# A stored normalised copy of the rows between the first spectral layer and the first convolution

## The chip, the core and the metric

The kernel runs on one core of a Trainium2 chip. Its time is the device time of one execution in microseconds (us). The engines of the core run their own instruction queues: TensorE (PE, matmuls; PEld is its weight loads), VectorE (DVE), ScalarE (ACT), GpSimd (POOL) and SyncE (SP), on whose queue nearly all DMAs are issued here. Each engine takes its instructions in order.

## The reference

Four layers act on x of 2048 rows by 512 columns, float32. Layers 1 and 3 are spectral, layers 2 and 4 are long convolutions along the rows, and each is added to its input.

```python
def _layernorm(x, axis=-1, eps=1e-5):
    m = jnp.mean(x, axis=axis, keepdims=True)
    v = jnp.var(x, axis=axis, keepdims=True)
    return (x - m) / jnp.sqrt(v + eps)
def _A_ref(x, w_r, w_i):
    X = rfft2(x)
    return irfft2(X * (w_r + 1j * w_i), s=(S, D))
def _B_ref(u, log_A_real, A_imag, C_real, C_imag, log_dt, D_skip):
    dt = exp(log_dt)
    A = -exp(log_A_real) + 1j * A_imag
    C = (C_real + 1j * C_imag) * dt[:, None]
    P = exp((A * dt[:, None])[:, :, None] * pos[None, None, :])
    K = 2.0 * einsum("dn,dnl->dl", C, P).real
    ...
    return y + u * D_skip[None, None, :]
x = x + _A_ref(_layernorm(x), ...)
x = x + _B_ref(_layernorm(x), ...)
x = x + _A_ref(_layernorm(x), ...)
x = x + _B_ref(_layernorm(x), ...)
```

`y` in `_B_ref` is the causal convolution of u with K, by FFTs of twice the length. K depends on the weights alone, and both convolution layers use the same.

## The kernel before

The 2048 rows lie as 128 partitions by 16 rows each, so that "a row" below is a tile of 128 x 512 (256 KB), and there are 16 of them (`n2` from 0 to 15). All transforms are matmuls with tables.

The first spectral layer (`layer_a` with `x=None`) has three parts. `spread` loads the rows, normalises them and transforms along the rows. `middle` transforms along the columns, multiplies with the weights w, and goes back. `end` folds (`fold`) and brings back each row (`rows_back`): the old row is loaded again into a tile `hr` (queue key R, L410), one matmul (L596) makes the layer's output, VectorE adds the two into `hr` (L602), and the sum is stored to an array `h1` in HBM (L604). Rows are taken in groups of 4, 4, 4, 2, 1, 1 (`LN` read from the back is their sizes), and for each group `layer_norm_stats` makes the mean and the inverse deviation: one BN_STATS (L341) and one BN_AGGR (L342) a row, then thirteen small VectorE instructions (L347 to L364, three Newton steps) that depend on each other almost throughout. They go to a small tile `norms` of 2 x 16 numbers per partition. The tile `hr` shares four buffers with the weight tile `wt` (`hr="wt"`, `WT = 4`).

The first convolution (`layer_b` with `src=hd`) works through four blocks of 128 columns. For each, `forward_norm` loads four rows' 128 columns at a time from `h1` into a tile `w` (key N, L1059), GpSimd scales and shifts each of the four with its numbers from `norms` (L1065, 64 steps in all), and `forward_b` transforms them: 32 matmuls per four rows (L318, through `side_by_side`), a copy by ScalarE (L643), and eight transposes by VectorE (L649) per block. `weigh` multiplies with the convolution kernel's spectrum (L954, L956, then sums L965 and L966 on GpSimd, mostly), `back` returns, and the sum with the rows of `h1` (L990 loads them, L994 adds) goes to `h2` or to the tile `za`, with the statistics of the next layer (L999).

Beside that, the convolution kernel itself is made: `kernel_time` builds K in time and stores it to `kt`, in groups of four units of two halves. Each half takes two matmuls, a rounding by VectorE (L833), a third matmul (L834), three ScalarE activations (L795: `kf`, then two sines into `qp`), three VectorE products (L852 twice, L854 once) and sixteen small matmuls (L865); a group begins with eight exponentials by ScalarE into `mag` (L795) of which GpSimd makes a third part (L816, L817), and ScalarE loads another table of functions before the sines and again before the exponentials. `kernel_freq` transforms K block by block, with the same `forward_b`, and its product is kept (`keep`, L919).

The order of the work on each engine is not written out. The program lists steps interleaved by shares (`interleave`, `FILL`, `FS`), and a planner that runs a timeline of its own orders each engine's instructions from that list; a step moves ahead when what stands before it would have to wait. Buffers are taken in rotation: a tile's next use waits until all readers of its earlier use are done.

Of the kernel before, what the change touches and what calls it, by code (L numbers as in the profile page):

```python
# [31 lines left out]
LAGE = 3  # L32
WT = 4
WA = 7
LN = '444211'
# [3 lines left out]
NEWT = 1  # L39
XNE = 'gggg'  # L40
GA = '22444'
# [22 lines left out]
S2 = 0  # L64
# [184 lines left out]
class Net:  # L249
# [134 lines left out]

    def layer_a(self, w, x=None, src=None, dst=None):

# [179 lines left out]
        def fold(n2):  # L566
            if n2 == 0:
                vs["tat"] = self.load("ta" if x is not None else TT, "tat", [16, 128])
                if x is not None:
                    self.xn = self.sb("x", [16, 512])  # L570
                else:
                    self.norms = self.sb("norms", [2, 16])
            p = self.ps("p3", [512])
# [19 lines left out]
        def rows_back(n2):  # L593
            old = row(n2, self.sb("hr", [512])) if x is None else x[:, n2]
            p = self.ps("p3", [512])
            nc.tensor.matmul(p, vs["tat"][:, n2], vs.pop(n2), start=True, stop=True)  # L596
            if not done:
                norm["sums"] = self.sb("lsum", [4], 2)
            if S2 if x is None else S3:
                self.add_up(old, old, p, norm["sums"][:, len(done):len(done) + 1])  # L600
            else:
                nc.vector.tensor_add(old, old, p)  # L602
            if x is None:
                self.dma("D")(dst[:, n2], old)  # L604
            done.append(old)
            if len(done) == sizes[-1]:
                sizes.pop()
                n = len(done)
                nr = self.layer_norm_stats(done, newton=x is None or NW[2] == "1", sums=norm["sums"][:, :n] if (S2 if x is None else S3) else None,
                                           nr=self.norms[:, :, n2 - n + 1:n2 + 1] if x is None else None)  # L610
# [323 lines left out]

    def layer_b(self, kf, T, out, x=None, src=None, first=None, more=(), fill=(), switch=(), kept=None, after=None):

# [30 lines left out]
        def back(blk, Y):  # L967
# [15 lines left out]
            def rows(n0):  # L983
# [13 lines left out]
                if src is not None:  # L997
                    for i in range(4):
# [3 lines left out]

        steps = [first or self.forward_norm(0, T, src)] + [self.forward_norm(blk, T, src, "z3" if more and blk == 3 else "z")
                                                           for blk in range(1, 4)]
# [44 lines left out]

    def forward_norm(self, blk, T, h=None, tag="z"):  # L1050

        ds = slice(128 * blk, 128 * blk + 128)
        rows = {}

        def src(n2):
            i = n2 % 4
            if i == 0:
                t = rows["t"] = self.sb("w", [4, 128])
                self.dma("N")(t, h[:, n2:n2 + 4, ds])  # L1059
                for k in range(4):  # L1060
                    scale, bias = (self.norms[:, c, n2 + k:n2 + k + 1] for c in (1, 0))
                    if XNE[k] == "a":
                        self.nc.scalar.activation(t[:, k], t[:, k], ACT.Identity, bias=bias, scale=scale)
                    else:
                        (self.nc.gpsimd if XNE[k] == "g" else self.nc.vector).tensor_scalar(  # L1065
                            t[:, k], t[:, k], scale, bias, op0=ALU.mult, op1=ALU.add)
            return rows["t"][:, i]

        return self.forward_b(src if h is not None else lambda n2: self.xn[:, n2, ds], T, tag)

# [5 lines left out]
def net_kernel(ctx, tc, x, w, ends, kin, log_dt, d_skip, out, **cst):  # L1076
# [14 lines left out]
    with ExitStack() as outer:  # L1091
        with ExitStack() as early:
            early.enter_context(net.phase("pk", P, pk=(2048, PK), pv=(2048, PV)))
            with net.phase("p", P, p1=(2048, 8 - PK - PV), p2="p1", p3="p1"), \
                    net.phase("a", x=(32768, 1), ta=(8192, 1), ca=(6912, 1), u=(16384, 2), w=(2056, WA), wt=(2056, WT), hr="wt",
                              wv="w", junk="w"):
                A = net.layer_a(w, src=xv, dst=hd)
                with net.phase("m", side="right", raw=(8192, 1), val=(10240, 1), tmp=(14336, 1), hp=(5120, 2)):
# [29 lines left out]
            F = [net.kernel_freq(blk, kt, d_skip, kf, kept, T) for blk in range(4)]  # L1128
            first = net.forward_norm(0, T, hd)
            at = cuts[1]  # L1130
# [25 lines left out]
            net.layer_b(kf, T, hd2, src=hd, first=first, more=[(2 * b - EF, F[b]) for b in range(EF, 4)],  # L1156
                        fill=[K[i:j] for i, j in zip(cuts, cuts[1:])], switch=[(SW, switch), (SW + 2, fetch)], kept=kept, after=after)
# [42 lines left out]
```

## Time and profile before

| | |
|---|---|
| three runs | 804.79, 809.13, 813.25 us (median 809.13) |
| the profiled execution | 813.32 us, of which 811.5 us are the span from the first to the last instruction |
| mean granted TensorE clock | 0.924 |
| DMA | 80.49 MB, of it 54.77 MB read from HBM and 25.03 MB written |

The profile names an instruction by its line (L602), engine, operation, what it writes and reads (`hr<-hr,p`), and shape. A row in order of time has its start, its duration in us, and in brackets for how long the engine had been idle and what ended that. An instruction's duration can reach into the next one's, since they are pipelined, so the distance between two starts is what a chain of them costs. A row of a table by stretch has the busy time and the number of instructions of each engine in the stretch. "Granted clock" is the share of TensorE's full clock that the throttle left. The three runs spread over 1%, and a difference is read against that.

### The profile page before, as it was taken

Reading aid. Unit: us, or ns where it says so; the run is one execution under the profiler, and the core shown is the slowest. Engines: PE = TensorE matmul, PEld = TensorE weight load, DVE = VectorE, ACT = ScalarE, POOL = GpSimd, SP = SyncE. Lnnn points to the kernel's source line nnn. Section 1 sums busy time; section 2 is a strip of 40 time slices with the busy share of each in tenths; the row PEclk is TensorE's granted clock in tenths of the full one; section 3 lists DMA queues with packets and bytes.
Section 4 is the critical chain, followed back from the end, with each engine's and each line's share of the span. In section 5 each row is a group of like instructions: output and inputs, shape, how many; then the busy total and the mean of one; then the engine's idle time right before and its main releaser. Section 6 shows DMA issues by size and latency. Waiting matters only on the chain. (4 is left out here: it accounts for less than half of the span.)

```text
span 811.5 us, 18861 instructions
## 1 busy us (share of the span) xinstructions
PE 640.9 (79%) x7231; PEld 450.0 (55%) x7232; DVE 644.8 (79%) x1307; ACT 428.4 (53%) x918; POOL 406.0 (50%) x594
## 2 busy tenths in 40 slices
PE   3448788896867977998689969665999896989895
PEld 2336666664534534654266637344877663566675
DVE  6998739789898979879796977657577796977971
ACT  2424769855548765786578714213766345323311
POOL 3675876755617054711574644180065661654752
PEclk9999989999978998999899989887999997999998
DMA  8200642253547322560335466302123013323511
GB/s 310 111 0 2 153 103 61 99 110 127 116 141 179 122 29 53 123 174 26 69 104 124 138 140 189 120 17 102 52 80 85 21 44 113 105 74 96 149 53 53
DMA packets 144609, 80.49 MB, mean 99 GB/s; under 512 B 78500, under 2 KB 124200, under 8 KB 143624
## 3 DMA queue, kind: packets, MB, share of 16 engines
q1 hardware_dynamic: 144264, 78.77, 34.6%
q8 instruction: 57, 0.93, 0.5%
q0 software_dynamic: 256, 0.52, 0.4%
q14 instruction: 32, 0.26, 0.1%
HBM read 54.77 MB, written 25.03 MB: 98 GB/s over the span
## 5 line engine op out<-in xcount | busy, mean ns | idle before, releaser
L966 POOL TENSOR_TENSOR u<-wb,wb 64x512 f32<-64x512 f32 x64 | 93.1, 1454 | 106.9 <-DVE wb L954 99.7
L318 PE MATMUL p<-z,mb 128*64 128x512 f32 (+1 forms) x480 | 105.7, 560 | 18.8 <-DVE z L649 10.4
L954 DVE TENSOR_TENSOR wb<-p,kk 128x512 f32<-128x512 f32 x128 | 80.8, 674 | 17.9 <-PE p L318 16.5
L318 PE MATMUL p<-mb,u 128*64 128x64 f32 x2048 | 78.5, 246 | 20.0 <-POOL u L965 19.5
L318 PEld LDWEIGHTS p<-mb,u 128*64 128x64 f32 x2048 | 75.2, 160 | 28.9 <-POOL u L965 23.3
L865 PE MATMUL pv<-qp 128*64 128x128 f32 x1024 | 77.8, 292 | 10.3 <-DVE qp L854 8.8
L865 PEld LDWEIGHTS pv<-qp 128*64 128x64 f32 x1024 | 61.1, 145 | 38.1 <-issue 16.8
L643 ACT COPY z<-p 128x512 f32<-128x512 f32 x96 | 51.8, 597 | 57.0 <-PE p L318 47.3
L854 DVE TENSOR_TENSOR qp<-qp,mag 128x1024 f32<-128x1024 f32 x64 | 80.4, 1260 | 0.9
L852 DVE SCALAR_TENSOR_TENSOR qp<-qp,mag 128x256 f32<-128x256 f32 x128 | 64.6, 522 | 16.6 <-ACT qp L795 16.5
L528 DVE TENSOR_TENSOR w<-wt,p 128x514 f32<-128x514 f32 x64 | 42.7, 687 | 35.8 <-PE p L318 25.6
L980 ACT COPY u<-p 128x512 f32<-128x512 f32 x64 | 37.4, 588 | 61.0 <-PE p L318 60.7
L318 PEld LDWEIGHTS p<-z,mb 128*64 128x64 f32 x480 | 37.6, 147 | 55.1 <-issue 25.1
L533 POOL TENSOR_TENSOR w<-w,w 64x257 f32<-64x257 f32 x48 | 40.4, 842 | 52.2 <-DVE w L528 47.4
L649 DVE STREAM_TRANSPOSE z<-z 128x512 f32<-128x512 f32 x96 | 58.3, 671 | 9.0 <-ACT z L643 9.0
L458 PE MATMUL p<-w,w 128*128 128x128 f32 x128 | 32.8, 438 | 40.8 <-DVE w L451 29.7
L1065 POOL TENSOR_SCALAR w<-w,norms 128x128 f32<-128x128 f32 x64 | 38.8, 619 | 37.8 <-DMA w<-h 19.2
L795 ACT ACTIVATE kf<-pk 128x512 f32<-128x512 f32 x64 | 38.9, 607 | 33.0 <-PE pk L834 30.9
L458 PEld LDWEIGHTS p<-w,w 128*128 128x128 f32 x128 | 28.5, 327 | 44.8 <-issue 23.9
L833 DVE TENSOR_SCALAR kw<-pk 128x512 bf16<-128x512 f32 x64 | 43.1, 680 | 8.2 <-PE pk L831 8.1
L795 ACT ACTIVATE qp<-kf,half 128x512 f32<-128x512 f32 x64 | 47.3, 738 | 0.1
L546 PE MATMUL p<-ca,w 128*128 128x128 f32 x256 | 41.5, 294 | 7.3 <-DVE w L535 2.5
(198 smaller groups left out, 1533.0 us busy)
## 6 DMA issues: line engine op xcount, KB each, us to landing
wt<-in_w SPq DMA_DIRECT2D x32, 257.0 KB
w<-h SPq DMA_DIRECT2D x32, 256.0 KB
kf<-kk SPq DMA_DIRECT2D x32, 256.0 KB
kk<-kf SPq DMA_DIRECT2D x32, 256.0 KB
u<-in_x SPq DMA_DIRECT2D x16, 256.0 KB
hr<-in_x SPq DMA_DIRECT2D x16, 256.0 KB
kt<-stage SPq DMA_DIRECT2D x32, 128.0 KB
h<-hr SPq DMA_DIRECT2D x16, 256.0 KB
```

Source lines behind the costliest of these rows:

```text
L318: last = self.nc.tensor.matmul(out, weights, data, start=True, stop=True, skip_group_check=True).ins
L458: nc.tensor.matmul(p[:, b], xf[:, b], t, start=True, stop=True)
L528: nc.vector.tensor_mul(m[pl], W, px[:, None, :].to_broadcast([128, 2, 257]))
L643: nc.scalar.copy(tiles["z"][:, :, :, b, m:m + 2].rearrange("p u j m r -> p (u j) (m r)"), ps[b].rearrange("p u j m r -> p (u j) (m r)"))
L649: nc.vector.transpose(tiles["zt"][:, u:u + 8].rearrange("p u j d -> p (u j d)"), tiles["z"][:, u:u + 8].rearrange("p u j b m r -> p (u j b ...
L795: last["x"] = nc.scalar.activation(*a, **k).ins
L833: nc.vector.tensor_scalar(whole, p, MAGIC, -MAGIC, op0=ALU.add, op1=ALU.add)
L852: nc.vector.scalar_tensor_tensor(QP[:, c, 0], QP[:, c, 1, :, ::-1], -1.0 if c else 1.0, m[:, 0], op0=ALU.mult, op1=ALU.mult)
L854: nc.vector.tensor_mul(t, t, mag[:, None, 1:3, 256 * j:256 * j + 256].to_broadcast([128, 2, 2, 256]))
L865: nc.tensor.matmul(p[64 * t:64 * t + 64, g], QP[:, c, 2, d:d + 2].rearrange("p s a -> p (s a)"), QP[:, c, 0:2, d:d + 2].rearrange("p k s b ...
L954: nc.vector.tensor_mul(split(m[c, pl], "du", [32, 16]), by_channel(p), split(k[c], "du", [32, 16]))
L966: e[1].tensor_add(y[64:128], v[0, 1], v[1, 0])
```

## The change

The numbers of a row's norm are applied where they are made. In the first spectral layer ScalarE writes `scale * row + bias` for each row of a group into a tile `xr` (128 x 512, two buffers), which a DMA stores to a new array `hn` in HBM; the other spectral layer did this before, into a tile that stays on the chip. The first convolution's `forward_norm` then loads from `hn` instead of `h1`, and GpSimd's 64 steps are gone, with the tile `norms`. The sums are still stored to `h1` and loaded from there for the addition. The tile `hr` gets seven buffers of its own.

```diff
+HR = 7
-XNE = 'gggg'
...
             if len(done) == sizes[-1]:
                 sizes.pop()
                 n = len(done)
-                nr = self.layer_norm_stats(done, ..., nr=self.norms[:, :, n2 - n + 1:n2 + 1] if x is None else None)
-                if x is not None:
-                    for i in range(n):
-                        nc.scalar.activation(self.xn[:, n2 - n + 1 + i], done[i], ACT.Identity,
-                                             bias=nr[:, 0, i:i + 1], scale=nr[:, 1, i:i + 1])
+                nr = self.layer_norm_stats(done, ...)
+                for i in range(n):
+                    k_ = n2 - n + 1 + i
+                    y = self.sb("xr", [512]) if x is None else self.xn[:, k_]
+                    nc.scalar.activation(y, done[i], ACT.Identity, bias=nr[:, 0, i:i + 1], scale=nr[:, 1, i:i + 1])
+                    if x is None:
+                        self.dma("D")(norm_dst[:, k_], y)
                 done.clear()
...
         def src(n2):
-            i = n2 % 4
-            if i == 0:
-                t = rows["t"] = self.sb("w", [4, 128])
-                self.dma("N")(t, h[:, n2:n2 + 4, ds])
-                for k in range(4):
-                    scale, bias = (self.norms[:, c, n2 + k:n2 + k + 1] for c in (1, 0))
-                    if XNE[k] == "a":
-                        self.nc.scalar.activation(t[:, k], t[:, k], ACT.Identity, bias=bias, scale=scale)
-                    else:
-                        (self.nc.gpsimd if XNE[k] == "g" else self.nc.vector).tensor_scalar(
-                            t[:, k], t[:, k], scale, bias, op0=ALU.mult, op1=ALU.add)
-            return rows["t"][:, i]
+            if n2 % 4 == 0:
+                rows["t"] = self.sb("w", [4, 128])
+                self.dma("N")(rows["t"], xn[:, n2:n2 + 4, ds])
+            return rows["t"][:, n2 % 4]
...
-    hd, hd2 = (net.dram.tile([128, 16, 512], F32, name=n) for n in ("h1", "h2"))
+    hd, hd2, hn = (net.dram.tile([128, 16, 512], F32, name=n) for n in ("h1", "h2", "hn"))
...
-                    net.phase("a", ..., w=(2056, WA), wt=(2056, WT), hr="wt",
+                    net.phase("a", ..., w=(2056, WA), wt=(2056, WT), hr=(2048, HR), xr=(2048, 2),
```

The planner orders anew what the change touches. The line numbers in its rows are those of the kernel that they belong to: L602, L833, L852, L854, L795, L604, L787 of before are L600, L832, L851, L853, L794, L602, L786 of the changed kernel. The first place is VectorE at the row additions of the first spectral layer. Before, the thirteenth and the fourteenth addition of the sixteen stand close together, with a little of the convolution kernel's making around them:

```order
L602 TENSOR_TENSOR hr_601_2460<-hr_601_2460,p1_602_2462 128x512
L833 TENSOR_SCALAR kw_410_1766<-pk_411_1767 128x512
L852 SCALAR_TENSOR_TENSOR qp_408_1758<-qp_408_1758,mag_365_1594 128x256 x2
L602 TENSOR_TENSOR hr_606_2477<-hr_606_2477,p1_607_2479 128x512
L342 BN_AGGR bmv_585_2404<-bst_589_2414 128x2
L583 TENSOR_TENSOR w_599_2453<-p1_597_2446,w_598_2451 128x256
L584 TENSOR_TENSOR w_599_2453<-p1_597_2446,w_598_2451 128x256
L833 TENSOR_SCALAR kw_420_1803<-pk_421_1804 128x512
```

Now the twelfth addition stands behind the end of the second group's norm (`lnn_544`) and behind a whole group of the convolution kernel's making (`qp_475` is its last):

```order
L853 TENSOR_TENSOR qp_475_2009<-qp_475_2009,mag_389_1694 128x2x512
L360 SCALAR_TENSOR_TENSOR lnr_551_2286<-lnt_552_2287,lnr_551_2286 128x4
L358 SCALAR_TENSOR_TENSOR lnt_552_2287<-lnr_551_2286 128x4
L359 TENSOR_TENSOR lnt_552_2287<-lnt_552_2287,lnv_550_2285 128x4
L360 SCALAR_TENSOR_TENSOR lnn_544_2271<-lnt_552_2287,lnr_551_2286 128x4
L364 SCALAR_TENSOR_TENSOR lnn_544_2271<-bmv_545_2272,lnn_544_2271 128x4
L600 TENSOR_TENSOR hr_592_2424<-hr_592_2424,p1_593_2426 128x512
L832 TENSOR_SCALAR kw_557_2313<-pk_558_2314 128x512
```

What moved is the addition, later by more than twenty pieces of L852 for the last row; counted over the whole order, 28 of the 128 instructions of L852 (L851) stand ahead of the seventh row addition in both, 40 and now 64 ahead of the last, and 51 and now 88 ahead of the first transpose. The second place is ScalarE at the exponentials (`mag`) of a group of the convolution kernel's making. Before they stand among copies of the fold (L580) and of K's sums (L873):

```order
L795 ACTIVATE mag_385_1683<-pk_388_1690 128x512
L580 COPY w_553_2303<-p1_552_2298 128x256
L795 ACTIVATE mag_389_1693<-pk_390_1694 128x512
L795 ACTIVATE mag_389_1693<-pk_392_1700 128x512
L873 COPY stage_319_1376<-pv_383_1662 128x128x2
```

Now the normalisations of a group of four rows stand among those of the next group, ahead of the table load and the first sine:

```order
L611 ACTIVATE xr_553_2301<-hr_501_2106,lnn_544_2271 128x512
L611 ACTIVATE xr_554_2304<-hr_515_2164,lnn_544_2271 128x512
L872 COPY stage_435_1864<-pv_517_2170 128x128x2
L794 ACTIVATE mag_530_2231<-pk_533_2238 128x512
L794 ACTIVATE mag_534_2241<-pk_535_2242 128x512
L611 ACTIVATE xr_555_2307<-hr_527_2218,lnn_544_2271 128x512
L872 COPY stage_435_1864<-pv_522_2190 128x128x2
L794 ACTIVATE mag_534_2241<-pk_537_2248 128x512
L611 ACTIVATE xr_556_2310<-hr_542_2265,lnn_544_2271 128x512
L794 ACTIVATE kf_560_2320<-pk_558_2314 128x512
L794 ACT_TABLE_LOAD
```

What moved is the norm's application, into ScalarE's queue ahead of the sines that VectorE works on next. The third place is SP's queue at the end of the first spectral layer. Before, the last store of a sum is followed by the load of the convolution's transform table `t`:

```order
L604 DMA h1_63<-hr_601_2460 128x512
L604 DMA h1_63<-hr_606_2477 128x512
L410 DMA hr_628_2558<-in_x 128x512
L604 DMA h1_63<-hr_616_2511 128x512
L604 DMA h1_63<-hr_628_2558 128x512
L307 DMA t_638_2600<-in_t 128x2048
```

Now the stores of normalised rows stand there, with loads of the convolution kernel's making (`th`) between them, and `t` behind the last:

```order
L613 DMA hn_65<-xr_606_2469 128x512
L786 DMA th_829_3553<-parts_61 48x1x256 x2
L613 DMA hn_65<-xr_629_2546 128x512
L786 DMA th_829_3553<-parts_61 48x1x256 x2
L613 DMA hn_65<-xr_630_2549 128x512
L786 DMA th_829_3553<-parts_61 48x1x256 x2
L613 DMA hn_65<-xr_642_2585 128x512
L786 DMA th_840_3605<-parts_61 48x1x256 x6
L613 DMA hn_65<-xr_656_2636 128x512
L307 DMA t_659_2654<-in_t 128x2048
```

What moved is the table's load, from behind the last sum to behind the last normalised row.

More of the change, by code (lines that the diff above doesn't have):

```diff
@@ L570, in fold @@
                     self.xn = self.sb("x", [16, 512])
-                else:
-                    self.norms = self.sb("norms", [2, 16])
             p = self.ps("p3", [512])
@@ L608, in rows_back @@
                 n = len(done)
-                nr = self.layer_norm_stats(done, newton=x is None or NW[2] == "1", sums=norm["sums"][:, :n] if (S2 if x is None else S3) else None,
-                                           nr=self.norms[:, :, n2 - n + 1:n2 + 1] if x is None else None)
-                if x is not None:
-                    for i in range(n):
-                        nc.scalar.activation(self.xn[:, n2 - n + 1 + i], done[i], ACT.Identity,
-                                             bias=nr[:, 0, i:i + 1], scale=nr[:, 1, i:i + 1])
+                nr = self.layer_norm_stats(done, newton=x is None or NW[2] == "1", sums=norm["sums"][:, :n] if (S2 if x is None else S3) else None)
+                for i in range(n):
[4 more added lines that the diff above has]
+                        self.dma("D")(norm_dst[:, k_], y)
                 done.clear()
@@ L933, in kernel_freq, with layer_b @@
         return rows, turns, [partial(keep, i) for i in range(4)]
-    def layer_b(self, kf, T, out, x=None, src=None, first=None, more=(), fill=(), switch=(), kept=None, after=None):
+    def layer_b(self, kf, T, out, x=None, src=None, xn=None, first=None, more=(), fill=(), switch=(), kept=None, after=None):
         nc = self.nc
@@ L1001, in back @@
             return [partial(units, j, d) for j in range(2) for d in range(0, 32, 8)], [partial(rows, n0) for n0 in range(0, 16, 4)]
-        steps = [first or self.forward_norm(0, T, src)] + [self.forward_norm(blk, T, src, "z3" if more and blk == 3 else "z")
+        steps = [first or self.forward_norm(0, T, xn)] + [self.forward_norm(blk, T, xn, "z3" if more and blk == 3 else "z")
                                                            for blk in range(1, 4)]
@@ L1128, in net_kernel @@
             F = [net.kernel_freq(blk, kt, d_skip, kf, kept, T) for blk in range(4)]
-            first = net.forward_norm(0, T, hd)
+            first = net.forward_norm(0, T, hn)
             at = cuts[1]
@@ L1155, in net_kernel @@
                 cuts[i:] = [max(c, marks[8 * b + 7]) for c in cuts[i:]]
-            net.layer_b(kf, T, hd2, src=hd, first=first, more=[(2 * b - EF, F[b]) for b in range(EF, 4)],
+            net.layer_b(kf, T, hd2, src=hd, xn=hn, first=first, more=[(2 * b - EF, F[b]) for b in range(EF, 4)],
                         fill=[K[i:j] for i, j in zip(cuts, cuts[1:])], switch=[(SW, switch), (SW + 2, fetch)], kept=kept, after=after)
```

11 lines of the change are left out of this document (5 added, 6 removed).

## The prediction, on record before the changed kernel ran

> **What bounds the kernel now.** I read the page's busy shares first, then the groups by line, then the busy time by stretch, and last the time-ordered rows of VectorE (DVE) and ScalarE (ACT). The busy shares (engine, us, share, instructions) show two engines level and none full:
>
> ```profile
> span 811.5 us, 18861 instructions
> PE 640.9 (79%) x7231; PEld 450.0 (55%) x7232; DVE 644.8 (79%) x1307; ACT 428.4 (53%) x918; POOL 406.0 (50%) x594
> ```
>
> So an average decides nothing, and the step that is removed sits on POOL, the idlest of these. Its row (one line's instructions, then who waited for them):
>
> ```profile
> L1065 POOL TENSOR_SCALAR w<-w,norms x64: 443/450/2891, 253.9 to 467.3; 128x128 f32<-128x128 f32 x64
> ...
> who waited for it (us, times):
>   PEld p L318: 0.6, 2
> ```
>
> The 64 norm steps lie between 253.9 and 467.3 us, and the matmuls that read them waited 0.6 us. Three landmarks on DVE (start, us, instruction): the first and the seventh row addition of the first spectral layer, and the first transposes of the convolution:
>
> ```profile
> 168.43 0.69 DVE L602 TENSOR_TENSOR hr<-hr,p 128x512 f32<-128x512 f32 x1 [1.10 <-PE p L596]
> ...
> 195.33 0.67 DVE L602 TENSOR_TENSOR hr<-hr,p 128x512 f32<-128x512 f32 x1
> ...
> 264.68 0.69 DVE L649 STREAM_TRANSPOSE z<-z 128x512 f32<-128x512 f32 x1
> ```
>
> Each forward transform ends in eight such transposes; they alternate between a block of the convolution kernel (F) and a block of normalised rows (N). The busy time by stretch, cut at the seventh row addition and then at the starts of these groups F, N, F, N, F, N, N (stretch, length, then busy us of PE, PEld, DVE, ACT and POOL, granted clock, DMA share, GB/s):
>
> ```profile
> 195.30:264.70 69.40, 50.80 (x442) 30.65 (x442) 63.88 (x174) 42.99 (x80) 36.75 (x56) 0.86 0.53 144
> 264.70:285.70 21.00, 20.43 (x237) 10.72 (x234) 19.19 (x37) 17.53 (x36) 0.00 (x0) 0.97 0.35 116
> 285.70:337.40 51.70, 40.48 (x477) 24.34 (x477) 45.70 (x68) 33.73 (x64) 28.80 (x24) 0.90 0.31 70
> 337.40:374.90 37.50, 35.73 (x552) 24.44 (x550) 30.28 (x63) 29.21 (x58) 10.45 (x21) 1.00 0.46 120
> 374.90:427.60 52.70, 39.37 (x436) 21.64 (x432) 45.07 (x67) 33.98 (x64) 31.50 (x27) 0.87 0.30 68
> 427.60:466.80 39.20, 37.68 (x571) 26.34 (x570) 32.64 (x67) 30.77 (x61) 20.46 (x32) 1.00 0.51 136
> 466.80:492.00 25.20, 18.58 (x271) 10.11 (x270) 19.98 (x31) 6.20 (x13) 13.48 (x13) 0.86 0.77 177
> ```
>
> From 195 to 265 us, the end of the first spectral layer, DVE is the limit (63.88 of 69.40, 5.5 idle). In the two stretches from N to F (51.70 and 52.70) it is DVE again, with 45 us; in the three from F to N (21.00, 37.50, 39.20) PE is within 5% of full. POOL is nowhere the fullest. What fills all of these is the making of the convolution kernel in time (here called K: lines L787 to L877), independent work that the planner slips between. The last stretch has none left; it weighs a block and transforms the next, as those from N to F do, and is only 25.20 long.
>
> **What the change moves.** The order of the built program shows more than the diff: 128 K instructions of line L852 run on DVE in all. Ahead of the seventh row addition stand 28 in both kernels; ahead of the last row addition 40 before and 64 now; ahead of the first transposes 51 before and 88 now. In the five stretches that follow stood 11, 18, 14, 18, 16 and stand now 8, 10, 9, 13, 0. The cause is the buffer of a row: before, it was free once its sum was stored and its statistics read; now it is free only when ACT has normalised it, which waits for thirteen small DVE instructions on its group of rows. With seven buffers, the eighth row waits for the first group of four, and the planner fills each such wait with K. So 37 pieces of K move from the convolution to ahead of it.
>
> *K ahead of the convolution, longer.* The pitch of K on DVE, from starts of neighbours in a stretch where nothing waits:
>
> ```profile
> 241.88 0.68 DVE L833 TENSOR_SCALAR kw<-pk 128x512 bf16<-128x512 f32 x1
> 242.48 1.21 DVE L854 TENSOR_TENSOR qp<-qp,mag 128x1024 f32<-128x1024 f32 x1
> 243.61 0.15 DVE L359 TENSOR_TENSOR lnt<-lnt,lnv 128x4 f32<-128x4 f32 x1
> ...
> 244.89 0.75 DVE L852 SCALAR_TENSOR_TENSOR qp<-qp,mag 128x256 f32<-128x256 f32 x2
> 245.56 0.15 DVE L360 SCALAR_TENSOR_TENSOR lnr<-lnt,lnr 128x4 f32<-128x4 f32 x1
> ```
>
> One L833 (0.60), one L854 (1.13) and two L852 (0.67) make 2.40 us, so 1.20 per L852: 37 x 1.20 = **+44.4 us**. K comes in groups of 16 L852, and between two groups DVE waits for ACT:
>
> ```profile
> 248.97 1.21 DVE L854 TENSOR_TENSOR qp<-qp,mag 128x1024 f32<-128x1024 f32 x1
> ...
> 256.80 1.27 DVE L833 TENSOR_SCALAR kw<-pk 128x512 bf16<-128x512 f32 x2
> 260.55 0.43 DVE L852 SCALAR_TENSOR_TENSOR qp<-qp,mag 128x256 f32<-128x256 f32 x1 [2.47 <-ACT qp L795]
> ```
>
> From the end of that L854's pitch (250.10) to 260.55 are 10.45 us, here nearly filled by small norm instructions. ACT did three pairs of copies of 1.07 each in it:
>
> ```profile
> 250.17 1.07 ACT L643 COPY z<-p 128x512 f32<-128x512 f32 x2 [0.28 <-PE p L318]
> ...
> 258.01 0.60 ACT L795 ACTIVATE kf<-pk 128x512 f32<-128x512 f32 x1 [1.56 <-PE pk L834]
> 258.62 1.28 ACT L795 ACT_TABLE_LOAD   x1
> ```
>
> Without those copies a gap is about 7 us. Four gaps now stand between the seventh row and the first transposes, and 11 of the 16 new ACT normalisations stand in them, each estimated at 0.5 (the start-to-start time of ACT's 128x512 forms, half of the 1.07 pair): 4 x 7 + 5.5 = 33.5. What the order gives DVE to do inside them (counted in rows at 0.60 for a 512-wide, 0.33 for a 256-wide and 0.15 for a small one) is about 19. That leaves 14.5 idle, against the 5.5 of the stretch from 195 us before: **+9 us**. Bounds: all filled, 0; gaps of 10.45 each, +22.
>
> *A new wait.* The normalised row has two buffers, so ACT's third row of a group waits until the first is stored in HBM; behind it on ACT stand K's exponentials, and behind the store on SP's queue row loads and K's loads. No row shows this store. The nearest is SP's own wait for the stored sum, where a row buffer is taken again:
>
> ```profile
> SPq L410 <- DMA h<-hr: 8.4, 6, 2.8
> ```
>
> That is in total, times, longest: 1.4 mean, 2.8 at most. Three groups of three or more rows: 3 x 1.4 = **+4 us**, from 0 to 3 x 2.8 = 8.4.
>
> *K out of the convolution, shorter.* From N to F, 18 L852 cost 51.70 - 25.20 = 26.5 us, 1.47 each. So (8 + 5) x 1.47 = **-19 us**. From F to N, PE is the limit, and what K takes of PE counts:
>
> ```profile
> 250.05 1.09 PE L865 MATMUL pv<-qp 128*64 128x128 f32 x16
> 251.08 0.61 PE L820 MATMUL pk<-kb,th 96*128 96x512 bf16 x2
> 251.62 1.10 PE L318 MATMUL p<-t,w 64*64 64x128 f32 x32
> ...
> 253.90 0.27 PE L830 MATMUL pk<-kb,th 96*128 96x256 bf16 x1
> 254.01 0.27 PE L831 MATMUL pk<-kb,th 96*128 96x256 bf16 x1
> ```
>
> 1.03 + 0.27 + 2 x 0.11 = 1.52 for two L852, 0.76 each (L834 left out, so a lower end); the upper end is DVE's 1.20. I take 1.00, between them since both engines are near full: (3 + 5 + 16) x 1.00 = **-24 us**, bounds -18 and -29.
>
> *Covered, at nothing.* The 64 POOL steps: only 0.6 us of waits hang on them. The 16 stores of 256 KB: the DMA engines are 0.53 busy in the 69.40 us row. SP's 16 more issues: 0.33 each by the row below, 5.3 us on a queue without arithmetic. The earlier loads of seven rows: the first is needed at 168.43, and a load more or less before that is no limit there. Both kernels have the same DVE instructions.
>
> ```profile
> L604 SPq DMA_DIRECT2D h<-hr x16: 319/333/2037, 169.1 to 237.3; - x16
> ```
>
> Should the 4 us above be exceeded, K's loads behind the stores are late next, and DVE idles. Behind the last stretch shown the order is the same but for stray rows: 0.
>
> **The sum**: 44.4 + 9 + 4 - 19 - 24 = +14 us. The profiled execution took 813.32 us, near the top of the three runs (804.79 to 813.25, median 809.13). The difference is set on the median: 809 + 14 = **823 us**.
>
> **The rivals.** (1) *K is neutral where it moves*: norm work fills every gap and no store is waited for: 44.4 - 19 - 29 = -4 to 44.4 - 19 - 18 = +7, so 805 to 816. For it: DVE is 92% busy from 195 to 265 already. Against: the order leaves bare K there. (2) *The POOL step was on the path*, faster: each of 16 groups of four rows goes load, POOL, matmul; were its 4 x 0.45 = 1.8 us exposed every time, 28.8 us would go against the +14, giving 794. It decides from 13 exposed groups on (14 + 8 = 22 us). Against: 0.6 us of waits. (3) *POOL holds DVE up while it runs*, faster: 64 x 0.45 = 28.8 us of DVE would come free, 809 + 14 - 29 = 794. Against it stand these rows:
>
> ```profile
> 247.08 0.62 POOL L816 TENSOR_TENSOR e<-mag 128x16 f32<-128x16 f32 x1 [16.96 <-ACT mag L795]
> ...
> 421.50 6.43 POOL L1065 TENSOR_SCALAR w<-w,norms 128x128 f32<-128x128 f32 x7 [1.84 <-DMA w<-h]
> ...
> 422.61 1.21 DVE L854 TENSOR_TENSOR qp<-qp,mag 128x1024 f32<-128x1024 f32 x1
> ```
>
> Beside POOL's steps DVE's L854 keeps the 1.21 us that it has at 242.48, in the 16.96 us in which POOL was idle, and POOL gives way (6.43 / 7 = 0.92 a step, 0.45 in the median). The Trainium skill, SBUF — State Buffer, section "SBUF: two separate sides", says that a DVE instruction with two SBUF inputs and a GpSimd instruction need one shared port pair, and that whichever starts first holds it for its whole instruction; by it DVE would gain here, which the trace bears out for POOL's side alone. (4) *The stores stall K*: gaps at their +22, waits at 8.4, savings at their lower ends: 44.4 + 22 + 8.4 - 19 - 18 = +38, so 847; from +22 on (831) I count it here. That the change does not do what it says is excluded: the order has none of POOL's 64 steps left, and 16 on ACT with 16 stores.
>
> **How the numbers follow.** The forecast (817 to 831) 0.44, rival 1 0.31, rival 2 0.08, rival 3 0.04, rival 4 0.13. The range 804 to 838 leaves out rivals 2 and 3 and the upper half of rival 4, under 0.2. About 1% (8 us) is what a measurement of this kernel can tell from no change: faster 0.12, within it 0.31, slower 0.57.
>
> **What would show it.** Right: the first group of transposes starts near 322 instead of 264.7 (44.4 + 13 later), K's last L852 comes before the third N transposes, and the sixth stretch, then without K, takes about 23 us instead of 39.20; ACT shows waits at the third row of a group; DVE's idle grows between 195 and 322. Wrong: first transposes before 312 (rival 1), L854 below 1.13 at the pitch (rival 3), N-to-F stretches shorter than 1.47 per L852 explains (rival 2), or DVE waits on loads of `th` (rival 4). The step least sure is the saving from F to N, since no F-to-N stretch without K was seen.

## The result: 849.9 us, slower by 4.9%

| | before | after |
|---|---|---|
| median of four runs each | 811.19 us (804.79 to 814.05) | 849.88 us (848.28 to 852.94) |
| after / before | | 1.0493, 95% interval 1.0419 to 1.0567 |
| span of the profiled execution | 811.5 us | 848.1 us |
| pieces of K (L852, now L851) ahead of the first transposes | 51 | 88 |

The sign was forecast, the size was not: 823 us, with a range up to 838. The profiled execution of the kernel before (813.32 us) lies at the slow end of its runs, so that sums by the two traces come out some 2 us smaller than the difference of the medians, 38.7. The granted clock does not make the difference: its mean was 0.877 in the profile of the changed kernel and 0.924 in that of before, but a run of the changed kernel at 0.897 took 848.28 us, and runs of the kernel before at 0.892 and 0.899 took 810.87 and 813.23. The page of the changed kernel, its busy shares (engine, us, share, instructions):

```profile
span 848.1 us, 18830 instructions
PE 651.9 (77%) x7232; PEld 455.9 (54%) x7232; DVE 637.5 (75%) x1307; ACT 441.8 (52%) x934; POOL 365.2 (43%) x530
```

No engine does more than a few per cent more than before, so the 36.6 us of span are idle time, or work that no longer lies beside other work. The landmarks on DVE in order of time: the first, the seventh and the last row addition, and the first transposes, which stood at 168.43, 195.33, 236.60 and 264.68 before. The first row is of before, its last addition; the others are of the changed kernel:

```profile
236.60 0.68 DVE L602 TENSOR_TENSOR hr<-hr,p 128x512 f32<-128x512 f32 x1
...
164.72 0.69 DVE L600 TENSOR_TENSOR hr<-hr,p 128x512 f32<-128x512 f32 x1 [1.10 <-PE p L594]
...
191.62 0.67 DVE L600 TENSOR_TENSOR hr<-hr,p 128x512 f32<-128x512 f32 x1
...
283.51 0.69 DVE L600 TENSOR_TENSOR hr<-hr,p 128x512 f32<-128x512 f32 x1 [1.46 <-DMA hr<-in_x]
...
334.95 1.90 DVE L648 STREAM_TRANSPOSE z<-z 128x512 f32<-128x512 f32 x3 [1.84 <-ACT z L642]
```

Up to the seventh addition the kernels agree but for 3.7 us. Then the additions come late, the last by 47 us, and they wait for the old row (`hr<-in_x`), which ended no wait of theirs in the kernel before. The busy time by stretch, with the cuts and columns of the prediction's table:

```profile
191.60:335.00 143.40, 101.96 (x784) 59.39 (x782) 108.82 (x248) 103.36 (x188) 37.31 (x56) 0.79 0.46 116
335.00:357.40 22.40, 20.47 (x230) 11.47 (x230) 15.07 (x29) 17.84 (x34) 0.88 (x2) 0.92 0.33 115
357.40:395.80 38.40, 32.95 (x437) 20.47 (x437) 36.05 (x53) 22.79 (x46) 22.52 (x19) 0.91 0.38 88
395.80:430.30 34.50, 31.14 (x462) 20.87 (x463) 22.81 (x54) 26.73 (x50) 5.16 (x8) 0.95 0.46 120
430.30:472.20 41.90, 31.34 (x408) 17.97 (x406) 35.94 (x57) 19.33 (x38) 21.25 (x12) 0.91 0.23 48
472.20:509.70 37.50, 27.09 (x422) 20.24 (x419) 12.47 (x35) 12.09 (x22) 0.00 (x0) 0.82 0.75 218
509.70:531.00 21.30, 18.18 (x267) 10.76 (x268) 19.11 (x31) 6.28 (x13) 13.35 (x10) 0.85 0.46 111
```

The first row is 74.0 us longer than before: DVE does 44.9 more in it (108.82 - 63.88) and idles 29.1 more (34.6 against 5.5). The two stretches from N to F (38.40 and 41.90) are shorter by 24.1 together. Of the three from F to N the sixth row is the one to look at: no K is left in it, DVE is busy for 12.47 instead of 32.64, and it still takes 37.50 instead of 39.20. The three together give back 3.3 us.

What a late addition waits for is seen at the twelfth, in an excerpt of all engines in order of time:

```profile
242.29 0.16 DVE L364 SCALAR_TENSOR_TENSOR lnn<-bmv,lnn 128x4 f32<-128x4 f32 x1
...
243.97 1.51 ACT L611 ACTIVATE xr<-hr,lnn 128x512 f32<-128x512 f32 x2
...
244.81 0.33 SPq L613 DMA_DIRECT2D hn<-xr  x1
245.18 0.42 SPq L410 DMA_DIRECT2D hr<-in_x  x1
...
248.22 0.69 DVE L600 TENSOR_TENSOR hr<-hr,p 128x512 f32<-128x512 f32 x1 [5.76 <-DMA hr<-in_x]
```

The norm of the second group is known at 242.45. ACT, which has a copy and two exponentials ahead of it, normalises from 243.97 on; a buffer is free with that, its new row is loaded from 245.18 on, and the addition starts at 248.22. DVE idles all the while, since the addition is next in its order.

### The profile page after: what moved, and what is told of

Same layout as the page of the kernel before. It is cut to its first block, busy times and chain, and to the rows that moved or that the text cites. A ratio compares the mean times of both kernels' runs of the same rounds, so it can differ in the third digit from the quotient of the medians.

```text
span 848.1 us, 18830 instructions
## 1 busy us (share of the span) xinstructions
PE 651.9 (77%) x7232; PEld 455.9 (54%) x7232; DVE 637.5 (75%) x1307; ACT 441.8 (52%) x934; POOL 365.2 (43%) x530
## 5 line engine op out<-in xcount | busy, mean ns | idle before, releaser
L965 POOL TENSOR_TENSOR u<-wb,wb 64x512 f32<-64x512 f32 x64 | 95.1, 1486 | 142.8 <-DVE wb L953 135.8
L864 PE MATMUL pv<-qp 128*64 128x128 f32 x1024 | 85.6, 315 | 14.6 <-ACT stage L872 4.2
L318 PE MATMUL p<-mb,u 128*64 128x64 f32 x2048 | 76.7, 244 | 24.4 <-POOL u L964 22.2
L864 PEld LDWEIGHTS pv<-qp 128*64 128x64 f32 x1024 | 66.9, 158 | 51.1 <-ACT stage L872 20.6
L853 DVE TENSOR_TENSOR qp<-qp,mag 128x1024 f32<-128x1024 f32 x64 | 80.8, 1267 | 0.7
L815 POOL TENSOR_TENSOR e<-mag 128x16 f32<-128x16 f32 x32 | 10.9, 341 | 153.7 <-ACT mag L794 153.5
L851 DVE SCALAR_TENSOR_TENSOR qp<-qp,mag 128x256 f32<-128x256 f32 x128 | 55.6, 449 | 19.3 <-ACT qp L794 19.3
L458 PE MATMUL p<-w,w 128*128 128x128 f32 x128 | 31.6, 426 | 40.8 <-DVE w L451 30.4
L318 PE MATMUL p<-t,w 64*64 64x128 f32 x1024 | 47.0, 293 | 10.7 <-DMA w<-kt 7.1
L318 PEld LDWEIGHTS p<-t,w 64*64 64x64 f32 x1024 | 34.1, 142 | 31.1 <-issue 14.0
L832 DVE TENSOR_SCALAR kw<-pk 128x512 bf16<-128x512 f32 x64 | 43.0, 680 | 9.4 <-PE pk L830 9.2
L794 ACT ACTIVATE kf<-pk 128x512 f32<-128x512 f32 x64 | 38.5, 602 | 19.7 <-PE pk L833 19.4
```

The source lines that it names most:

```text
L318: last = self.nc.tensor.matmul(out, weights, data, start=True, stop=True, skip_group_check=True).ins
L458: nc.tensor.matmul(p[:, b], xf[:, b], t, start=True, stop=True)
L832: nc.vector.tensor_scalar(whole, p, MAGIC, -MAGIC, op0=ALU.add, op1=ALU.add)
L851: nc.vector.scalar_tensor_tensor(QP[:, c, 0], QP[:, c, 1, :, ::-1], -1.0 if c else 1.0, m[:, 0], op0=ALU.mult, op1=ALU.mult)
L853: nc.vector.tensor_mul(t, t, mag[:, None, 1:3, 256 * j:256 * j + 256].to_broadcast([128, 2, 2, 256]))
L864: nc.tensor.matmul(p[64 * t:64 * t + 64, g], QP[:, c, 2, d:d + 2].rearrange("p s a -> p (s a)"), QP[:, c, 0:2, d:d + 2].rearrange("p k s b ...
```

## The experiments

Three theories. **1**: a row buffer, held until its row is normalised, makes the additions late, and K is put into the waits. **2**: the two buffers of the normalised row, its stores, and SP's queue. **3**: ScalarE's 16 normalisations. Each run was compared with runs of the kernel before on the same chip; ratios are to those, with 95% intervals.

*Places for all rows (rows16), more places for normalised rows (xr5), both.* The spectrum's tile `x` is dead when the rows are loaded again, so 16 rows fit there.

```diff
-TT = 'x'
+TT = 'ta'
...
+                t = self.sb("x", [16, 512])
...
+                    vs["hr"] = t
...
-            old = row(n2, self.sb("hr", [512])) if x is None else x[:, n2]
+            old = row(n2, vs["hr"][:, n2]) if x is None else x[:, n2]
```

> The changed kernel, but all 16 rows of the first spectral layer have a place of their own (in the space of the spectrum, which is dead by then; the transform's table moves to the first table's space). In the order, pieces of K ahead of the first transposes fall from 88 to 64 (51 in the kernel before). Theory 1 (a row buffer held until ACT has normalised it makes the additions late, and K is put into the waits): the last addition comes back to about 237 us instead of 283.5, and the time goes with the pieces: 38.7 us for 37 pieces is 1.05 each, 13 pieces left, so 811 + 14 = about 825. Theory 2 (the two buffers of the normalised row and the stores on SP's queue): additions stay late, 845 to 853. Theory 3 (ACT's 16 normalisations at 0.80 = 13 us, on top of whatever else): not under 824.

Measured 823.5 us, ratio 1.0179 (1.0122 to 1.0236). The rows of DVE for the last addition and the first transposes:

```profile
232.76 0.68 DVE L603 TENSOR_TENSOR x<-x,p 128x512 f32<-128x512 f32 x1
...
290.51 1.89 DVE L651 STREAM_TRANSPOSE z<-z 128x512 f32<-128x512 f32 x3
```

The additions are on time again, as theory 1 has it, with the normalisations, the stores and the two buffers of `xr` all in place: two thirds of the loss (26 of 39 us) are gone.

```diff
-                    net.phase("a", ..., hr=(2048, HR), xr=(2048, 2),
+                    net.phase("a", ..., hr=(2048, HR), xr=(2048, 5),
```

> The changed kernel with five buffers for the normalised row instead of two; row buffers stay seven. In the order 80 pieces of K stand ahead of the first transposes instead of 88. Theory 1: 29 pieces more than before, 811 + 29 x 1.05 = about 841; the last addition stays later than 270 us. Theory 2: the waits of ACT for the stores go (6.6 us in 6 waits) and with them most of the loss, 811 to 820. Theory 3: no change, 850.

Measured 839.5 us, ratio 1.0381 (1.0326 to 1.0435); the last addition stays at 284.5. Theory 1's number. The buffers of `xr` are worth some 10 us, probably since waiting for one prolongs the hold on a row, and are not the main cause.

Both edits together, with nine buffers, for which the seven of `hr` leave the space:

```diff
-                    net.phase("a", ..., hr=(2048, HR), xr=(2048, 2),
+                    net.phase("a", ..., xr=(2048, 9),
```

> Both: 16 places for rows and nine buffers for the normalised row. 62 pieces of K ahead of the first transposes. Theory 1: 811 + 11 x 1.05 = about 823, near the run with 16 rows alone. Theory 2: 811 to 820, and far from the run with 16 rows alone. Theory 3 (ACT): 824 at least. If the change is free once no buffer holds anything up: 806 to 814.

Measured 817.9 us, ratio 1.0102 (1.0036 to 1.0167): the cheapest form of the change that was found, and not faster than before.

*POOL's norm steps by themselves (before_raw).* Edit: the loop over `k` in `src` of `forward_norm` is left out.

> The kernel before without POOL's 64 norm steps: the convolution transforms the rows without normalising them (this part of the computation is left out). DVE's order is that of the kernel before. Worth of the POOL steps: my prediction has them at nothing, so 809 to 813, within 0.5% of before; if they were on the path (rival 2) 783 to 790; if POOL held DVE up through a shared port (rival 3) about 783, with DVE's three-operand K instruction shorter than 1.21 us.

Measured ratio 0.9973 (0.9935 to 1.0012): the steps that the change removes cost nothing that can be told from the spread. L854, which by rival 3 would be shorter without them, keeps its mean (1256 ns, 1260 before). Rivals 2 and 3 of the prediction fall with it.

*The hold alone (before_hold), and a tighter one (rows4).*

```diff
-                    net.phase("a", ..., hr="wt",
+                    net.phase("a", ..., hr=(2048, 7),
...
+                if x is None:
+                    for i in range(n):
+                        nc.scalar.activation(self.sb("one", [1], 2), done[i][:, 0:1], ACT.Identity,
+                                             bias=nr[:, 0, i:i + 1], scale=nr[:, 1, i:i + 1])
```

> The kernel before, with seven row buffers of their own, and after each group's statistics ScalarE reads one column of each of its rows with the norm's factors (into a scratch column that nothing uses; some 0.2 us each). So a row buffer is held until the norm is known, as in the changed kernel, but there is no normalisation in that layer, no extra array and no store of it; POOL's norm steps stay. In the order 82 pieces of K stand ahead of the first transposes (51 before, 88 after). Theory 1 (the held buffer is the cause): 811 + 31 x 1.05 = about 843, first transposes near 320 us. Theories 2 and 3 (stores; ScalarE's 13 us): 809 to 815. Should POOL's steps or the moved loads matter besides, it lies between.

Measured 846.2 us, ratio 1.0450 (1.0382 to 1.0519). Its row for the stretch from the seventh addition to the first transposes:

```profile
191.90:321.20 129.30, 91.52 (x750) 53.77 (x750) 103.59 (x235) 92.00 (x180) 45.44 (x72) 0.83 0.42 95
```

Without a normalisation in that layer, its stores or an array, holding the buffers costs nearly what the whole change does: 129.30 us where before had 69.40, 25.7 of them DVE idle. A read of one column took 0.38 us, more than the 0.2 expected. The seven buffers of their own were not tried without the reads; but the next run, with fewer of them, is slower, so having more is not what costs time.

```diff
-HR = 7
+HR = 4
```

> The changed kernel with four row buffers instead of seven: each group of four rows can be added only after the group before is normalised. 96 pieces of K ahead of the first transposes. Theory 1: 811 + 45 x 1.05 = about 858. Theories 2 and 3: no change, 850.

Measured 855.6 us, ratio 1.0568 (1.0508 to 1.0629), as theory 1 expected.

*The stores (after_no_store) and who normalises (rows16_xr9_norm_pool).* Edits: the line `self.dma("D")(norm_dst[:, k_], y)` is left out and `xn=hd` loaded; `nc.gpsimd.tensor_scalar(y, done[i], nr[:, 1, i:i + 1], nr[:, 0, i:i + 1], op0=ALU.mult, op1=ALU.add)` in place of the activation.

> The changed kernel with seven row buffers, without the stores of the normalised rows; the convolution loads the sums instead, so that its rows are not normalised (left out). 76 pieces of K ahead of the first transposes. Theory 1: 811 + 25 x 1.05 = about 837, last addition still near 283 us. Theory 2 (stores and their queue): 811 to 818.

Measured 839.0 us, ratio 1.0361 (1.0297 to 1.0424), the last addition at 276.0: theory 1 again, although the four runs spread wide (828.5 to 839.9). The pieces fall from 88 to 76 with the stores, so these are worth some 11 us, as the buffers of `xr` are.

> The run with 16 places for rows and nine buffers (817.9), but POOL normalises the rows in that layer instead of ScalarE. This prices ScalarE's 16 normalisations (16 x 0.80 = 13 us). 64 pieces of K ahead of the first transposes (62 with ScalarE). Theory 3 (ScalarE's time there is what is left of the loss): 806 to 811. Theory 1 (the pieces decide, 11 more than before with ScalarE, 13 with POOL): 818 to 824.

Measured 829.0 us, ratio 1.0274 (1.0221 to 1.0326), above what either theory gave. Taking the work off ScalarE gains nothing, so its time there is not shown to be what is left of the loss; what POOL's form costs besides was not separated.

*Two tries to beat the kernel before.* Edits: `DQ = 'Ng'` (row loads of the convolution on POOL's queue); besides, `LN = '4444'`.

> The run with 16 places for rows and nine buffers for the normalised row (817.9), and the convolution's loads of normalised rows on POOL's queue, which this kernel leaves idle. Order of VectorE unchanged. The same move took 2.6 us off the changed kernel (849.9 to 847.3), so about 815; if the loads wait for nothing here, 818. To beat the kernel before it would have to come under 803, which only a shorter path in every N block (four blocks by 4 us) would give.

Measured 822.6 us, ratio 1.0190 (1.0143 to 1.0237): no gain where 815 was expected.

> As the run before it in this call, and the rows' statistics in four groups of four instead of 4, 4, 4, 2, 1, 1: 38 small VectorE instructions fewer (1271 in all against 1309). The tail of the norms, some 17 us of small dependent instructions after the last addition, shrinks to one group's chain. Expected 808 to 813, if the tail is on the path; 815 if not, or more if the last group's wait for its fourth row costs what it saves.

Measured 837.6 us, ratio 1.0385 (1.0341 to 1.0429), a clear miss. The end of the first layer, from the seventh addition to the first transposes, is no shorter (94.4 us against 92.7 in the run before). K runs later, and its last six pieces fall into the seventh stretch of the tables, which was free of K and takes 43.5 us here instead of 26.7; why it grows by so much stays open. It shows that the count of pieces ahead of the convolution is not a price by itself.

*What sets the stretches from F to N.* First the queue in the changed kernel, again with all engines in order of time. DVE waits 11 us for the load of the last block's K, which stands ahead of the N transposes in its order, while the rows to be transposed are ready at 502.09. The load itself waits on SP's queue for a store out of the same tile (`h<-w`, 4.6 us). The kernel before has no such wait in this stretch. The rows of the changed kernel:

```profile
501.02 1.07 ACT L642 COPY z<-p 128x512 f32<-128x512 f32 x2 [1.19 <-PE p L318]
...
506.60 1.28 SPq L903 DMA_DIRECT2D w<-kt  x2
...
509.53 0.28 DVE L908 TENSOR_TENSOR w<-w,dsk 1x128 f32<-1x128 f32 x1 [11.06 <-DMA w<-kt]
509.74 0.69 DVE L648 STREAM_TRANSPOSE z<-z 128x512 f32<-128x512 f32 x1
```

Edit: `DQ = 'Ng'` in the changed kernel.

> The changed kernel; only the convolution's loads of normalised rows are issued from POOL's queue instead of SP's. VectorE's order is the same as in the changed kernel. On the stretch from the third F to the third N transposes, 37.5 us though without K where my prediction had 23: if SP's queue, on which a row load waits behind stores and loads of others (8.4 us in three waits) and the kernel's loads behind it (VectorE's 11.1 us on them), holds this stretch, it falls to about 30 and the kernel to about 842. If it is a chain of small steps between engines, it stays at 36 to 39 and the kernel at 847 to 853.

Measured 847.3 us, ratio 1.0460 (1.0405 to 1.0514), not to be told from the changed kernel's. The stretch takes 34.9 us, which lies between the two expectations; DVE still waits 7.3 us in it for that load of K's. Then half of K taken out of the kernel before:

```diff
-                K, marks = net.kernel_time(parts, kt, list(range(32)), GROUP)
+                K, marks = net.kernel_time(parts, kt, list(range(16)), GROUP)
...
-        ds = slice(128 * blk, 128 * blk + 128)
+        ds = slice(128 * (blk % 2), 128 * (blk % 2) + 128)
...
-FILL = [0.31, 0.45, 0.5, 0.69, 0.84, 0.99]
+FILL = [0.62, 0.9, 1, 1, 1, 1]
```

> The kernel before with half of K: the convolution kernel is made for the first two blocks of channels only, and blocks three and four use those (64 of 128 pieces left out). The order is the same up to the second N stretch; pieces in the stretches after the first transposes are 11, 2, 0, 0, 0 instead of 11, 18, 14, 18, 16. By my prediction's prices (1.47 a piece from N to F, 1.00 from F to N): F1-N1 falls from 37.6 to about 24, F2-N2 from 39.2 to 23, the two N-F stretches from 52 to 28 and 26, the kernel to about 730. If K costs nothing from F to N (a chain of steps sets their length): F1-N1 and F2-N2 stay at 36 to 39, the N-F stretches fall as before, the kernel comes to about 760.

Measured 752.4 us, ratio 0.9292 (0.9248 to 0.9335), nearer to the second expectation. Its rows for N0-F1 with two pieces of K, and for F1-N1, N1-F2 and F2-N2, all without K (the groups are counted from 0):

```profile
282.00:319.90 37.90, 24.55 (x344) 16.27 (x346) 20.88 (x35) 8.96 (x19) 18.86 (x16) 0.82 0.46 106
319.90:350.30 30.40, 23.65 (x388) 17.06 (x382) 12.34 (x34) 12.03 (x22) 5.23 (x12) 0.94 0.38 126
350.30:377.70 27.40, 19.30 (x282) 11.74 (x284) 20.18 (x32) 6.27 (x12) 16.72 (x12) 0.94 0.41 106
377.70:412.00 34.30, 26.01 (x418) 18.96 (x412) 12.48 (x35) 12.03 (x22) 13.94 (x32) 0.89 0.53 168
```

Fourteen pieces fewer take 12.1 us of work off PE (35.73 - 23.65) but 7.1 off the stretch; sixteen fewer take 11.7 off PE (37.68 - 26.01) and 4.9 off the stretch. PE, idle for under 2 us before, is idle for 6.8 and 8.3 now. In F2-N2 the same load of K as above ends the stretch (a row of ACT, then two of DVE):

```profile
407.01 1.07 ACT L643 COPY z<-p 128x512 f32<-128x512 f32 x2 [1.19 <-PE p L318]
...
411.82 0.28 DVE L909 TENSOR_TENSOR w<-w,dsk 1x128 f32<-1x128 f32 x1 [7.36 <-DMA w<-kt]
412.03 4.84 DVE L649 STREAM_TRANSPOSE z<-z 128x512 f32<-128x512 f32 x8
```

The rows are ready at 408.08, 30.4 us behind the stretch's start at 377.70, and F1-N1, where DVE waits for no load of K, takes 30.40 as well. So the floor is about 30 us in both, and the other 3.9 of the 34.30 are the wait for that load.

From N to F the two stretches differ: 18 pieces fewer are 25.3 us in N1-F2, 1.41 each, but 16 fewer are only 13.8 in N0-F1, 0.86 each, where 28 us were expected and 37.90 measured. DVE waits there 8.6 us for a load of K's (L909), and PE in turn 8.5 for DVE. Is the floor from F to N made by the loads of rows and POOL's steps? Edit: before_half_K without the loop over `k`, and `DQ = 'Ng'`.

> The kernel before with half of K (752.4), without POOL's norm steps (left out, so that rows are not normalised), and with the row loads of the convolution on POOL's idle queue. The two F-N stretches without K took 30.4 and 34.4 us there. If the row loads on SP's queue and POOL's steps set their length, they fall to about 24 (what TensorE is busy in them) and the kernel by 15 or so, to about 737. If the steps between TensorE, ScalarE and VectorE set it, they stay within 2 us of 30.4 and 34.4, and the kernel at 747 to 755.

Measured 750.8 us; ratio 0.9277 (0.9226 to 0.9329).

```profile
316.10:346.20 30.10, 23.33 (x386) 16.92 (x381) 12.36 (x35) 12.03 (x22) 0.75 (x1) 0.94 0.40 131
375.60:408.90 33.30, 23.45 (x416) 17.27 (x412) 12.47 (x35) 12.03 (x22) 3.72 (x5) 0.97 0.57 179
```

The floor of the first stays, so it is neither the loads of rows nor POOL's steps. The second still holds a wait of DVE for K's load, which stayed on SP's queue (8.0 us; the rows are ready at 404.28, 28.7 behind the start). What waits in the first of these two stretches (who for whom, us in total, times, longest):

```profile
DVE z L649 <- ACT z L643: 11.1, 2, 7.4
ACT z L643 <- PE p L318: 10.1, 4, 4.1
...
ACT kk L919 <- PE p L318: 5.7, 8, 3.2
DVE w L994 <- PE p L318: 4.3, 2, 2.2
```

No wait of PE or of DVE there is put down to a load, and PE's own waits end with ACT (2.1 us) and DVE (3.4). What is left is the chain of PE, ACT and DVE steps that wait for each other in turn, and K had filled its holes; no run shortens that chain to test it.

*Hold or ScalarE's queue?* In before_hold the reads also stand in ScalarE's queue, behind the norm. The same reads, with 16 places for the rows (rows16's edit in before_hold):

> The kernel before with the same reads of one column by ScalarE as in the run that held seven buffers (846), but all 16 rows have a place of their own, so that no row waits for them; the norm steps stay on POOL, there is no extra array. 64 pieces of K ahead of the first transposes (82 with seven buffers, 51 before). If the held buffer is the cause: additions on time (the last near 235 us), 811 + 13 x 1.05 = about 825, as with 16 rows in the changed kernel (823.5). If it is ScalarE's queue, on which the reads wait for the norm with K's activations behind them: 840 to 850, as with seven buffers.

Measured 823.2 us, ratio 1.0174 (1.0119 to 1.0230), the last addition at 233.51. With the reads in place and the waiting for a buffer gone, 23 of the 35 us are gone. The hold is the cause. The rest has the size of the 13 pieces that still stand ahead of the first transposes; the likely reason, not tried apart, is that the convolution's tiles lie where the rows are, and so wait for the last read of the last row.

*All runs with the whole of K, by the pieces ahead of the first transposes* (counted in the order of each):

| | pieces | ratio to before |
|---|---|---|
| before_raw | 51 | 0.9973 |
| rows16_xr9; with POOL's queue | 62 | 1.0102; 1.0190 |
| rows16; before_hold_rows16; rows16_xr9_norm_pool; rows16_xr9_ln4 | 64 | 1.0179; 1.0174; 1.0274; 1.0385 |
| after_no_store | 76 | 1.0361 |
| xr5 | 80 | 1.0381 |
| before_hold | 82 | 1.0450 |
| the change; with POOL's queue | 88 | 1.0493; 1.0460 |
| rows4 | 96 | 1.0568 |

But for rows16_xr9_ln4, the times rise with the pieces, whatever brought these there: some 1% for eight, over the whole table. Runs with the same count differ by up to 1%, so the count is a guide and no price.

## Why the prediction was right in sign and wrong in size

*The cause*: right. The order had shown the held buffer and the 37 pieces, and before_hold, rows4 and rows16 confirm both, over the whole span from 51 to 96 pieces.

*K longer ahead of the convolution, +44.4*: DVE's work there rose by 44.9.

*Gaps between groups of K, +9, and waits for the store, +4*: mis-sized, together 29.1 us more of DVE idle instead of 13. The term counted ScalarE's gaps between groups of K, filled by what DVE could do in them, and had 14.5 us idle in them. By the trace DVE waits 8.9 us for K's sines and 8.9 for K's matmuls, 17.8 together. It left out the round trip at each group of rows (norm, ScalarE, load, addition), during which DVE has nothing: 8.3 us of waits for old rows, 5.76 of them at the twelfth. It also left out waits for ScalarE's copies of the fold, 5.7 us where before had 2.1. A normalisation also took 0.81, not the 0.5 that I estimated. The waits for the store that ACT shows, 6.6 us, lie between the bounds of 0 and 8.4.

*From N to F, -19*: it gave back 24.1, for 13 pieces 1.85 each instead of 1.47. In before_half_K the two stretches gave 0.86 and 1.41. So a fixed price per piece does not hold here, and why the change gave back more stays open.

*From F to N, -24*: **the step that failed**. It gave back 3.3. The prediction read "PE is the limit, and what K takes of PE counts", and took 1.00 a piece. PE was full there because K filled it. Without K the chain needs about 30 us (30.4 twice in before_half_K), where the prediction forecast 23 for the sixth stretch. So a piece is worth 0.51 (7.1 / 14), or 0.55 (8.8 / 16) up to where the rows are ready, below the lower bound of 0.75 (18 us for 24 pieces). In the changed kernel's sixth stretch the rows are ready after 29.9 us (at 502.09), by the same floor; the other 7.6 of its 37.50 are the wait for the load of K's last block, for which the sum had no term. Of the 16 us forecast there, the floor takes about 7 and this wait 7.6. The first of the three stretches got 1.4 longer with three pieces fewer; the reason stays open.

*The rest* came out 10 us shorter: 3.7 up to the seventh addition, 3.9 in the stretch from 509.70, and 2.4 behind it. The sum by the trace: 44.9 + 29.1 - 24.1 - 3.3 - 10.0 = 36.6 us, the difference of the spans.

*POOL's steps at nothing*: right (before_raw). *Rival 4* named the time, 847, but its mechanism, stores that hold up K, is worth some 10 us (xr5, after_no_store).

*The Trainium skill's port rule*, SBUF — State Buffer, section "SBUF: two separate sides": rival 3 took from it that DVE would gain where POOL's steps go. No gain was seen in before_raw. Yet the rule itself, that whichever starts first holds the port for its whole instruction, agrees with the trace of the changed kernel where POOL starts first (all engines in order of time):

```profile
202.51 1.05 POOL L816 TENSOR_TENSOR mag<-mag,e 128x512 f32<-128x512 f32 x1
...
202.61 0.97 DVE L359 TENSOR_TENSOR lnt<-lnt,lnv 128x4 f32<-128x4 f32 x1
```

An instruction of 0.15 us elsewhere takes 0.97, and ends 0.02 us after POOL's does (203.58 and 203.56). Ten of the norm's instructions between 200 and 335 us are longer than 0.5 us, 6.7 us more than at 0.15 each; before has eight of them, with 5.4. All eighteen end 0.02 to 0.03 us after a TENSOR_TENSOR of POOL, among them three with one tensor input only (L347, L351, L352). In three of before's DVE's recorded start is up to 0.05 us ahead of POOL's, and DVE still comes out last, so by recorded starts the rule does not hold in these.

## What to carry to other kernels

A step moved ahead keeps its inputs alive until it has run: count how many of their buffers it holds, for how long, and what waits for one, before counting the step itself. Where independent work fills a stretch, the full engine is no proof that the stretch ends with it; what taking the filler out can give is bounded by the chain beneath, which a neighbour with little filler, or a run with half of it, shows; and a load that waits where the filler stood can end the stretch instead. And a removed step that nobody waits for is worth nothing, however often it runs.

## What the runs showed of the hardware

ScalarE takes 0.81 us for a 128x512 normalisation from SBUF with a scale and a bias per partition (L611, 798 to 815 ns in 16 of 16), where its copies of the same shape out of PSUM take 0.59. The same on POOL took 0.83 in the median (1.06 in the mean) as one instruction per row, less than the 4 x 0.45 = 1.80 that the four 128x128 steps per row of before take by their median. TensorE's granted clock was 1.00 in the two stretches of before in which K filled PE (37.50 and 39.20 us). Without K these had 0.94 and 0.89 in before_half_K, and the changed kernel's sixth stretch 0.82: in these traces, one of each kernel, a stretch that lost its filler did not get a faster clock in return.
